# Two-stage attention with a gated convolution on one core: x in two layouts, float32 scores in column strips, block transposes, and the output product turned around

## The chip, the core and the metric

The kernel runs on one core of a Trainium2 chip. A core has five engines with queues of their own: PE multiplies matrices into PSUM (its weight loads are shown as PEld), DVE (VectorE) and ACT (ScalarE) work on SBUF and PSUM, POOL (GpSimd) on SBUF, and SP mostly issues transfers. Sixteen DMA engines carry the transfers that SP and ACT issue. Engines wait for one another through semaphores. The metric is the device time of one launch in microseconds (us); what the host does with inputs and outputs ahead of and behind the launch isn't in it.

## What is computed

x has 4 batches of 12,800 tokens with 128 channels in float32. With 32 learnt queries a summary h is drawn from x (phase one), each token then attends to the 32 rows of h (phase two), and the result goes through a causal convolution gate of five taps and two 128 by 128 products:

```python
def mab(q, kv):
    s = scale * (q @ kv.transpose(0, 2, 1))
    s = s - s.max(-1, keepdims=True)
    a = np.exp(s)
    a /= a.sum(-1, keepdims=True) + 1e-09
    return a @ kv
h = mab(I, x)
x = mab(x, h)
...
for k in range(K):
    gate_pre += conv_w[k][None, None, :] * xp[:, k:k + S, :]
gate = 1.0 / (1.0 + np.exp(-gate_pre))
val = x @ w_val
return (gate * val @ w_out).astype(np.float32)
```

Since each token's result is a mix of 32 rows, the taps and w_val are folded into weights of 32 rows (`wst`), and what the convolution reads is the table of probabilities.

## The kernel before

Tokens are dealt out so that a partition holds 100 neighbouring ones. A batch is cut into seven chunks of 8, 12 or 16 tokens a partition. In phase one, x is loaded (`load`), split into two float16 parts (`split1` L188 on ACT, `split2` L200 on DVE), and transposed, mostly by DMA (`trans_dma` L206, L209), partly by PE in the first batch. The scores with the queries (`scores`, L255 to L259) take a 128 by 128 tile of x as weights and 32 or 64 columns of queries as the moving side, two or three products for each tile; maximum, exponent and a second split follow, then the sums with x (`h_mm`). The functions `prep0` to `prep8` make from them the weights `wst` and the output weights `wo` of the batch.

Phase two of a chunk has the scores against h (`c_mm`), maximum, subtraction, exponent, sum and normalization (`c_max` to `c_norm`, POOL for L492 and L515), and four copies or parts of the float16 probabilities side by side (`c_hi`, `c_lo`, `c_dup`). These are transposed by PE (`y_mm`, L553) or by DMA (`y_t`, L544) into y, whose 128 rows are four blocks of 32: the probabilities, their low part, and copies. Two transfers (L579, L580) make z, a shifted copy of y, so that four products cover five taps.

The work that ends in the output is cut into 100 slots of 512 tokens, 25 a batch. A slot has four float16 gate products (`f_gate`, L589; three read y, one z), a value product (`f_val`, L596), tanh on ACT (`f_tanh`, L602), a multiplication on DVE (`f_gv`, L607), four float32 output products of 128 columns with g as weights (`f_out`, L613), and a copy and a store on ACT (`f_store`, L619, L620).

The order comes from due times: each function is put on a list with a time in units of a slot of 3.22 and the list is sorted; a scheduler then places the instructions, with some of them pinned behind others. The table that decides where a slot's steps stand against the next slot's is `F2`, with the steps gate, tanh, value, multiplication, output, store:

```python
for f, fn in zip(F2, (f_gate, f_tanh, f_val, f_gv, f_out, f_store)):
    at(t + f * SLOT, fn, b, c, q)
...
F2 = [-0.3, 0.23, 0.08, 0.87, 1.56, 2.08]
```

Of the kernel before, what the change touches and what calls it, by code (L numbers as in the profile page):

```python
# [10 lines left out]
F16 = mybir.dt.float16  # L11
# [10 lines left out]
NB = 100  # L22
TAPS = 5
HALO = TAPS - 1
SX = 64.0
SI = 64.0
SE = 4096.0
SH = 64.0
# [4 lines left out]

@with_exitstack
def tile_kernel(ctx: ExitStack, tc: tile.TileContext, x, inducing, w_val, conv_w, w_out, out):
    nc = tc.nc
    B = x.shape[0]
    SCALE = 1.0 / math.sqrt(P)
    V, S, T, G = nc.vector, nc.scalar, nc.tensor, nc.gpsimd

    xv = x.rearrange("b (p i) c -> b p i c", i=NB)
    ov = out.rearrange("b (p i) c -> b p i c", i=NB)

    chunks = [(0, 8), (8, 12)] + [(20 + 16 * g, 16) for g in range(5)]
    NCK = len(chunks)

    const = ctx.enter_context(tc.tile_pool(name="const", bufs=1))
    px = ctx.enter_context(tc.tile_pool(name="px", bufs=BUFS["XFB"]))
    pxs = ctx.enter_context(tc.tile_pool(name="pxs", bufs=BUFS["X12"]))
    pxt = ctx.enter_context(tc.tile_pool(name="pxt", bufs=BUFS["XT"]))  # L50
    pb = ctx.enter_context(tc.tile_pool(name="pb", bufs=2))
    p1 = ctx.enter_context(tc.tile_pool(name="p1", bufs=1))
    p2 = ctx.enter_context(tc.tile_pool(name="p2", bufs=2))
    p3 = ctx.enter_context(tc.tile_pool(name="p3", bufs=BUFS["P4B"]))
# [7 lines left out]
    def ps(role, shape, dt=F32):  # L62
        tag = PTAG[role]
        return psum.tile(shape, dt, name=role, tag=tag, bufs=PBUF[tag])

    def eng(op, b, c):
        return V if (ENG0 if b == 0 and c < 2 else ENG)[op] == "V" else G

    def copy(e, dst, src):
        if e == "S":  # L70
            S.copy(dst, src)
        else:
            (V if e == "V" else G).tensor_copy(dst, src)  # L73

    anchor = {}

    def pinned(e):
        if PIN and e in anchor:
            return tc.issue_after(anchor[e].ins)
        return contextlib.nullcontext()  # L80

    c_ = {}
    tpn = [0]
    st = {}
    bat = [dict() for _ in range(B)]
    xf_ = {}
    ys = {}
    zs = {}

    def constants():  # L90
        warm = const.tile([P, 1], F32, name="warm")
        V.memset(warm, 0.0)
        S.activation(warm, warm, AF.Exp)
        ident = const.tile([P, P], F16, name="ident")
        make_identity(nc, ident)
        identf = const.tile([P, P], F32, name="identf")
        make_identity(nc, identf)
        ones = const.tile([P, P], F32, name="ones")
        V.memset(ones, 1.0)
        ind = const.tile([M, P], F32, name="ind")  # L100
        nc.scalar.dma_start(ind, inducing)
        it = ps("t", [P, 512])
        T.transpose(it[:, :M], ind, identf[:M, :M])
        indT = const.tile([P, M], F32, name="indT")
        V.tensor_scalar(indT, it[:, :M], SI, None, ALU.mult)
        i12 = const.tile([P, 2, M], F16, name="i12")
        V.tensor_copy(i12[:, 0, :], indT)
        V.tensor_tensor(i12[:, 1, :], indT, i12[:, 0, :], ALU.subtract)
        iw = const.tile([P, M], F32, name="iw")
        V.tensor_scalar(iw, indT, SX, None, ALU.mult)  # L110
        w4 = const.tile([P, TAPS + 2, 4, M], F16, name="w4")
        G.memset(w4, 0.0)
        c_.update(w4=w4, ident=ident, identf=identf, ones=ones, i12=i12, iw=iw)

    def sched_f64(name, srcs, t, dt):
# [3 lines left out]
        def start():  # L119
            w["raw"] = p2.tile([P, k], I64, name=name + "_raw", tag="e", bufs=BUFS["EB"])  # L120
# [4 lines left out]
            w["w4"] = p2.tile([P, 4, k], I32, name=name + "_w4", tag="g", bufs=BUFS["TB"])  # L125
# [19 lines left out]
        at(t - 4, start)  # L145
# [8 lines left out]
    def halves(c):  # L154
        n = chunks[c][1]
        return {8: [(0, 8)], 12: [(0, 6), (6, 6)], 16: [(0, 8), (8, 8)]}[n]

    def half(b, c, i, kind):
        k = chunks[c][1] // len(halves(c))
        return st[b, c, i // k * k, kind], i % k  # L160

    def w1(b, c):
        return (W1 if b else W10)[c]

    def w2(b, c):
        return (W2 if b else W20)[c]

    def full(b, c):
        return b == 0 and PE_T0[c] == 2

    def load(b, c, q, m):
        if full(b, c) and len(wide) < BUFS["X12"]:
            wide.append((c, q))
            xf = pxs.tile([P, 8, P], F32, name="xw", tag="x12")
            st[b, c, q, "x"] = xf
        else:
            xf = px.tile([P, 8, P], F32, name="xf", tag="xf")
            if full(b, c):
                st[b, c, q, "x"] = xf
        dma = (nc.sync, nc.scalar, nc.gpsimd)[LQ[min(b, 1)]]  # L180
        for i, i0, k in [(0, NB - HALO, HALO), (HALO, 0, HALO)] if c == 0 else [(0, chunks[c][0] + q - HALO, m)]:
            dma.dma_start(xf[:, i:i + k, :], xv[b, :, i0:i0 + k, :])
        xf_[b, c, q] = xf

    def split1(b, c, q, m):
        x12 = st[b, c, q, "x"] = pxs.tile([P, 2, 8, P], F16, name="x12", tag="x12")
        with pinned("S"):
            S.mul(x12[:, 0, :m], xf_[b, c, q][:, :m], SX)  # L188

    def split2(b, c, q, m):  # L190
        xf, x1, x2 = xf_[b, c, q][:, :m], st[b, c, q, "x"][:, 0, :m], st[b, c, q, "x"][:, 1, :m]
        if (XP0, XP1, XP, XP)[b][2 * c + (1 if q else 0)]:
            if (XP0, XP1, XP, XP)[b][2 * c + (1 if q else 0)] == 2:
                S.mul(xf, xf, SX)
            else:
                G.tensor_scalar(xf, xf, SX, None, ALU.mult)
            G.tensor_tensor(x2, xf, x1, ALU.subtract)
            return
        with pinned("V"):
            V.scalar_tensor_tensor(x2, xf, SX, x1, ALU.mult, ALU.subtract)  # L200

    def trans_dma(b, c, q, m):
        xT = st[b, c, q, "T"] = pxt.tile([P, 2, 8, P], F16, name="xT", tag="xT")
        x12 = st[b, c, q, "x"]
        if m == 8:
            nc.sync.dma_start_transpose(xT.rearrange("p e i t -> p (e i) t"), x12.rearrange("p e i c -> p (e i c)"))  # L206
        else:
            for e in range(2):
                nc.sync.dma_start_transpose(xT[:, e, :m, :], x12[:, e, :m].rearrange("p i c -> p (i c)"))  # L209

    def trans_pe(b, c, q, m, e):
        if e == 0:
            st[b, c, q, "T"] = pxt.tile([P, 2, 8, P], F16, name="xT", tag="xT")
        tp = ps(XR[tpn[0] % len(XR)], [P, 8, P], F16)
        tpn[0] += 1
        for i in range(m):
            T.transpose(tp[:, i, :], st[b, c, q, "x"][:, e, i, :], c_["ident"])
        st[b, c, q, e] = tp

    def trans_evac(b, c, q, m, e):  # L220
        dst = st[b, c, q, "T"][:, e, :m, :]
        if e == 0:
            S.copy(dst, st[b, c, q, e][:, :m, :])
        else:
            V.tensor_copy(dst, st[b, c, q, e][:, :m, :])

    def trans_full(b, c, q, k, m):
        if k == 0:
            st[b, c, q, "T"] = pxt.tile([P, 8, P], F32, name="xTw", tag="xT")
        tp = ps(XR[tpn[0] % len(XR)], [P, 4, P])  # L230
        tpn[0] += 1
        for i in range(m):
            T.transpose(tp[:, i, :], xf_[b, c, q][:, k + i, :], c_["identf"])
        st[b, c, q, k] = tp

    def evac_full(b, c, q, k, m):
        dst, src = st[b, c, q, "T"][:, k:k + m, :], st[b, c, q, k][:, :m, :]
        if XE[2 * c + (1 if q else 0)][k // 4] == "S":
            S.copy(dst, src)
        else:  # L240
            V.tensor_copy(dst, src)

    def pieces(c):
        n = chunks[c][1]
        return {8: [(0, 8)], 12: [(0, 6), (6, 6)], 16: [(0, 8), (8, 8)]}[n]

    def scores(sc, b, c, q, m, rhs, rhsw, wide):
        for i in range(m):
            xT, k = half(b, c, q + i, "T")
            if full(b, c):  # L250
                T.matmul(sc[:, i, :M], xT[:, k, :], rhsw, start=True, stop=True)
                continue
            hi, lo = xT[:, 0, k, :], xT[:, 1, k, :]
            if wide:
                T.matmul(sc[:, i, :], hi, rhs.rearrange("p a j -> p (a j)"), start=True, stop=False)  # L255
            else:
                T.matmul(sc[:, i, :], hi, rhs[:, 1, :], start=True, stop=False)  # L257
                T.matmul(sc[:, i, :], hi, rhs[:, 0, :], start=False, stop=False)  # L258
            T.matmul(sc[:, i, :M], lo, rhs[:, 0, :], start=False, stop=True)  # L259

    def begin(b):
# [4 lines left out]
        if any(full(b, c) for c in range(NCK)):  # L266
            G.memset(d["h"], 0.0)
# [12 lines left out]
    def s1_add(b, c, q, m):  # L280
        s1 = st[b, c, "s1"][:, q:q + m, :]
        if full(b, c):
            return
# [534 lines left out]
```

## Time and profile before

| what | us |
|---|---|
| median of 3 runs (453.49 to 461.64) | 456.55 |
| span of the profiled execution, first to last instruction | 452.9 |
| PE busy, 0 to 80 us of the span | 49.96 (granted clock 0.68) |
| PE busy, 80 to 160 | 66.15 (0.96) |
| PE busy, 160 to 240 | 61.33 (0.91) |
| PE busy, 240 to 320 | 65.46 (0.96) |
| PE busy, 320 to 400 | 71.13 (0.96) |
| PE busy, 425 to 445 | 18.09 (0.91) |

The profile gives for the profiled execution its span; a time of its own with launch and end is not among what it shows, so the span is set against the runs. In the first 80 us the first batch's phase one runs. Then the output slots of a batch run beside phase one of the next, and from about 425 us on only the last slots are left. A row of a timeline has the start in the span, the duration, engine, line, operation, output and inputs, the shape, and in brackets how long the engine had been idle and what ended that. Rows of groups have the count after an x, then the busy time and the mean of one in ns. The granted clock is PE's, as a share of full speed. A matmul's end is modelled; back-to-back starts tell its cost better than its duration.

### The profile page before, as it was taken

Reading aid. Unit: us, or ns where it says so; the run is one execution under the profiler, and the core shown is the slowest. Engines: PE = TensorE matmul, PEld = TensorE weight load, DVE = VectorE, ACT = ScalarE, POOL = GpSimd, SP = SyncE. Lnnn points to the kernel's source line nnn. Section 1 sums busy time; section 2 is a strip of 40 time slices with the busy share of each in tenths; the row PEclk is TensorE's granted clock in tenths of the full one; section 3 lists DMA queues with packets and bytes.
Section 4 is the critical chain, followed back from the end, with each engine's and each line's share of the span. In section 5 each row is a group of like instructions: output and inputs, shape, how many; then the busy total and the mean of one; then the engine's idle time right before and its main releaser. Section 6 shows DMA issues by size and latency. Waiting matters only on the chain.

```text
span 452.9 us, 11587 instructions
## 1 busy us (share of the span) xinstructions
PE 355.6 (79%) x4597; PEld 274.8 (61%) x4597; DVE 346.0 (76%) x778; ACT 269.3 (59%) x454; POOL 216.1 (48%) x267
## 2 busy tenths in 40 slices
PE   3677656778899757887598868978779898988795
PEld 3576544557776545666386646756558676755463
DVE  4998899889877757997857878998939998665231
ACT  6667343486667535767555656676756566665353
POOL 2269827465865024584627313594737435462000
PEclk9666655799999988999979997999979999999898
DMA  8999539899999999999999798999997856789853
GB/s 290 255 236 201 112 77 204 205 250 257 240 245 200 171 166 233 242 235 230 203 241 272 187 198 173 289 243 243 229 211 178 172 155 163 158 186 224 178 162 117
DMA packets 137397, 93.18 MB, mean 206 GB/s; under 512 B 114016, under 2 KB 114304, under 8 KB 137344
## 3 DMA queue, kind: packets, MB, share of 16 engines
q1 hardware_dynamic: 121952, 65.94, 73.4%
q10 hardware_dynamic: 15392, 26.50, 17.9%
q8 instruction: 36, 0.59, 0.6%
q14 instruction: 17, 0.14, 0.1%
HBM read 26.50 MB, written 26.21 MB: 116 GB/s over the span
## 4 chain that ended last, share of the span: by engine, by line
DMA 39%; PE 27%; DVE 14%; POOL 7%; ACT 6%; issue 5%; SPq 1%; ACTq 0%; POOLq 0%; DVEq 0%
DMA xT<-x 19%; DMA z<-y 8%; PE g L589 7%; PE o L613 7%; DMA y<-p 6%; DMA out_dram<-os 4%; DVE x L200 2%; DVE g L607 2%; DMA xf<-in_x_dram 2%; PE v L596 2%; PE yp L553 2%; PE s L259 2%; ACT g L602 2%; PE s L255 1%; ACT x L188 1%
## 5 line engine op out<-in xcount | busy, mean ns | idle before, releaser
L613 PEld LDWEIGHTS o<-wo,g 128*128 128x128 f32 x800 | 106.5, 198 | 20.3 <-ACT os L619 7.3
L613 PE MATMUL o<-wo,g 128*128 128x128 f32 x800 | 114.2, 286 | 2.8 <-ACT os L619 1.7
L607 DVE SCALAR_TENSOR_TENSOR g<-g,v 128x512 f32<-128x512 f32 x100 | 67.7, 677 | 44.4 <-ACT g L602 33.6
L602 ACT ACTIVATE g<-g,gsc 128x512 f32<-128x512 f32 x100 | 68.8, 688 | 51.9 <-PE g L589 40.0
L619 ACT COPY os<-o 128x512 f32<-128x512 f32 x100 | 58.6, 586 | 56.2 <-PE o L613 41.7
L589 PE MATMUL g<-y,wst 128*128 128x512 f16 x296 | 83.0, 392 | 1.5 <-ACT g L602 1.5
L200 DVE SCALAR_TENSOR_TENSOR x<-xf,x 128x1024 f16<-128x1024 f32 (+1 forms) x51 | 70.8, 1396 | 1.0 <-ACT x L188 1.0
L589 PEld LDWEIGHTS <-wst 128*128 128x128 f16 x408 | 38.1, 100 | 46.6 <-DMA z<-y 17.5
L259 PEld LDWEIGHTS <-xT 128*128 128x128 f16 x800 | 59.2, 99 | 8.6 <-issue 4.2
L492 POOL TENSOR_TENSOR e<-e,m 128x512 f32<-128x512 f32 (+2 forms) x28 | 29.5, 1054 | 67.2 <-DVE m L486 61.7
L257 PE MATMUL s<-i,xT 128*128 128x32 f16 x356 | 33.9, 181 | 30.0 <-DMA xT<-x 28.9
L515 POOL TENSOR_TENSOR e<-e,z 128x512 f32<-128x512 f32 (+2 forms) x28 | 32.1, 1147 | 49.9 <-DVE z L507 33.2
L188 ACT ACTIVATE x<-xf 128x1024 f16<-128x1024 f32 (+1 forms) x52 | 52.1, 1019 | 5.7 <-DMA xf<-in_x_dram 5.5
L257 PEld LDWEIGHTS <-xT 128*128 128x128 f16 x404 | 33.1, 99 | 34.8 <-DMA xT<-x 32.1
L589 PE MATMUL g<-z,wst 128*128 128x512 f16 x92 | 36.2, 394 | 15.7 <-DMA z<-y 15.7
L530 POOL TENSOR_TENSOR p<-e,p 128x512 f16<-128x512 f32 (+2 forms) x28 | 36.4, 1301 | 19.2 <-DVE p L73 17.3
L596 PE MATMUL v<-y,wst 128*128 128x512 f16 x96 | 37.4, 390 | 6.1 <-DVE g L607 6.0
L307 POOL TENSOR_TENSOR s<-s,mb 128x512 f32<-128x512 f32 (+2 forms) x26 | 34.6, 1332 | 11.9 <-DVE mb L302 11.8
L255 PE MATMUL s<-h,xT 128*128 128x64 f16 x384 | 32.6, 196 | 3.3 <-DVE h L412 3.3
L258 PEld LDWEIGHTS <-xT 128*128 128x128 f16 x404 | 33.0, 99 | 3.0 <-issue 1.2
L259 PE MATMUL s<-i,xT 128*128 128x32 f16 x362 | 33.8, 180 | 0.3 <-DMA xT<-x 0.3
L258 PE MATMUL s<-i,xT 128*128 128x32 f16 x356 | 33.7, 180 | 0.0
(159 smaller groups left out, 763.5 us busy)
## 6 DMA issues: line engine op xcount, KB each, us to landing
out_dram<-os ACTq DMA_DIRECT2D x100, 256.0 KB, 4.0
xf<-in_x_dram SPq DMA_DIRECT2D x40, 512.0 KB, 5.4
z<-y SPq DMA_DIRECT2D x40, 256.0 KB, 4.4
xf<-in_x_dram SPq DMA_DIRECT2D x8, 384.0 KB, 4.5
xf<-in_x_dram SPq DMA_DIRECT2D x8, 256.0 KB, 4.2
z<-y SPq DMA_DIRECT2D x8, 192.0 KB, 4.1
xT<-x SPq DMA_TRANSPOSE x52, 5.8
y<-p SPq DMA_TRANSPOSE x11, 7.5
```

The source lines that it names most:

```text
L188: S.mul(x12[:, 0, :m], xf_[b, c, q][:, :m], SX)
L200: V.scalar_tensor_tensor(x2, xf, SX, x1, ALU.mult, ALU.subtract)
L255: T.matmul(sc[:, i, :], hi, rhs.rearrange("p a j -> p (a j)"), start=True, stop=False)
L257: T.matmul(sc[:, i, :], hi, rhs[:, 1, :], start=True, stop=False)
L258: T.matmul(sc[:, i, :], hi, rhs[:, 0, :], start=False, stop=False)
L259: T.matmul(sc[:, i, :M], lo, rhs[:, 0, :], start=False, stop=True)
L589: T.matmul(gp, d["wst"][:, k, :], r[:, q + o:q + o + 4, :].rearrange("p i t -> p (i t)"), start=i == 0, stop=i == len(taps) - 1)
L596: T.matmul(vp, d["wst"][:, 6, :], y[:, HALO + q:HALO + q + 4, :].rearrange("p i t -> p (i t)"), start=True, stop=True)
L602: anchor["S"] = S.activation(g, st[b, c, q, "g"], AF.Tanh, scale=bat[b]["gsc"])
L607: anchor["V"] = V.scalar_tensor_tensor(g, g, 1.0, st[b, c, q, "v"], ALU.add, ALU.mult)
L613: T.matmul(op[:, i, :], st[b, c, q, "gv"][:, i, :], bat[b]["wo"], start=True, stop=True)
L619: S.copy(os, st[b, c, q, "o"])
```

## The change

x is handed over twice: `xt` with channels in rows and tokens in columns, and `xk` in tiles of 128 tokens by 128 channels. The output is written with channels in rows. The layouts are made on the host. There are no splits and no transposes of x on the chip any more.

A batch is now six units of 2,048 tokens and one of 512. In both phases the scores are float32 products with the 32 queries (or the 32 rows of h) as weights and 512 tokens as the moving side; the four quarters of a unit go to four strips of 32 columns of PE, so that the result has queries and quarters in its 128 rows (`a_mm`, `b_mm`). In phase one maximum and sum are then along a row, the exponents are transposed by PE (`a_tr`) and multiplied with `xk`, again in four strips (`a_h`). In phase two DVE transposes blocks of 32 by 32 to get the queries along the row (`b_tr`) and back (`b_back`). The high and low float16 parts are laid into y by 16 transfers of 32 partitions a unit (`y_hi`, `y_lo`), and two more make z. The output product has `wo` as weights and 512 tokens as moving side, one product in place of four, and a store takes two slots.

There is no scheduler: the sorted list is the order on each engine, written out (`manual_schedule`). One unit of time is a slot. `LEAD` puts the scores of phase two six slots ahead of the slots that need them, and phase one of the next batch is spread among the slots of this one.

```diff
-    def f_out(b, c, q):
-        op = ps("o", [P, 4, P])
-        for i in range(4):
-            T.matmul(op[:, i, :], st[b, c, q, "gv"][:, i, :], bat[b]["wo"], start=True, stop=True)
-        st[b, c, q, "o"] = op
...
+    def a_mm(b, u):
+        w = UNITS[u][1]
+        sc = st[b, u, "s1"] = ps("s1", "s", [P, 512])
+        x = st[b, u, "xT"]
+        for g in range(G):
+            T.matmul(sc[M * g:M * g + M, :w], c_["iw"], x[:, w * g:w * g + w], start=True, stop=True, tile_position=(0, M * g))
...
+        for i in range(w // P):
+            T.transpose(et[:, i, :], st[b, u, "E"][:, P * i:P * i + P], c_["identf"])
...
+        for i in range(n):
+            for g in range(G):
+                T.matmul(hp[M * g:M * g + M, :], et[:, i, M * g:M * g + M], x[:, n * g + i, :],
+                         start=i == 0, stop=i == n - 1, tile_position=(0, M * g))
...
+    def b_mm(b, u):
+        w = UNITS[u][1]
+        sc = st[b, u, "s2"] = ps("s2", "s", [P, 512])
+        x = st[b, u, "xT"]
+        for g in range(G):
+            T.matmul(sc[M * g:M * g + M, :w], bat[b]["hq"], x[:, w * g:w * g + w], start=True, stop=True, tile_position=(0, M * g))
...
+    def b_tr(b, u):
+        w = UNITS[u][1]
+        s = st[b, u, "q"] = p2.tile([P, 16, M], F32, name="q", tag="q", bufs=3)
+        V.transpose(s[:, :w // M, :].rearrange("p i j -> p (i j)"), st[b, u, "s2"][:, :w])
...
+    def y_hi(b, u):
+        w = UNITS[u][1]
+        y, h = st[b, u, "y"], st[b, u, "hi"]
+        for blk, o in ((0, 4), (2, 4), (3, 6)):
+            for g in range(G):
+                nc.sync.dma_start(y[M * blk:M * blk + M, o + w * g:o + w * g + w], h[M * g:M * g + M, :w])
...
+        nc.sync.dma_start(z[:64, :n], y[:64, 0:n])
+        nc.sync.dma_start(z[64:, :n], y[:64, 1:n + 1])
...
+    def c_tanh(b, c):
+        g = st[b, c, "t"] = p2.tile([P, 512], F32, name="g", tag="gt", bufs=3)
+        S.activation(g, st[b, c, "g"], AF.Tanh, scale=bat[b]["gsc"])
...
+    def c_out(b, c):
+        op = st[b, c, "o"] = ps("o", "o", [P, 512])
+        T.matmul(op, bat[b]["wo"], st[b, c, "t"], start=True, stop=True)
...
+        for dt, fn in zip(CT, (c_gate, c_tanh, c_val, c_gv, c_out, c_ev)):
+            at(t + dt, fn, b, c)
...
+    with tc.manual_schedule():
...
+PBUF = dict(s=2, e=1, h=1, g=2, v=1, o=1)
+BUFS = dict(XT=10, XK=3, Y=3, Z=2, OS=2)
+LEAD = 6.0
...
+CT = [0, 0.3, 0.1, 0.6, 0.9, 1.25]
```

The order of PE at a slot's end, before. g_7182 are the gates of this slot; g_7175 is what tanh made of the gates of the slot ahead (g_7164):

```order
L589 MATMUL g_7182<-z4_7095,wst_6293 128x512
L596 LDWEIGHTS wst_6293
L596 MATMUL v_7191<-y_7074,wst_6293 128x512
L613 MATMUL o_7195<-wo_6299,g_7175 128x128 x4
L589 LDWEIGHTS wst_6293
L589 MATMUL g_7200<-y_7132,wst_6293 128x512
```

The output product reads what belongs to the slot ahead, and one slot's gates lie between a slot's own gates and its output product. The same place on PE in the new kernel; g_787 is what tanh makes of g_775, the gates just above:

```order
L372 MATMUL g_775<-zz_719,wst_485 128x512
L377 LDWEIGHTS wst_485
L377 MATMUL v_782<-y_664,wst_485 128x512
L389 MATMUL o_795<-g_787,wo_489 128x512
L372 LDWEIGHTS wst_485
L372 MATMUL g_797<-y_664,wst_485 128x512
```

The output product now reads its own slot's tanh and stands ahead of the next gates. Some slots have score work of the new kernel at this place on PE (s1 of the next batch's phase one, s2 of a later unit's phase two, four strips each):

```order
L377 LDWEIGHTS wst_485
L377 MATMUL v_817<-y_664,wst_485 128x512
L147 MATMUL s1_821<-xT_593,iw_99 32x512 x4
L389 MATMUL o_836<-g_828,wo_489 128x512
L285 MATMUL s2_838<-xT_118,hq_438 32x512 x4
L372 LDWEIGHTS wst_485
L372 MATMUL g_843<-y_664,wst_485 128x512
```

The s1 strips stand between value and output product, the s2 strips between the output product and the next gates. On SP a stretch of the middle of a batch reads like this before, where xT are transposes of x and z4 the shifted copy of y:

```order
L182 DMA xf_3680<-in_x_dram 128x1024
L579 DMA z4_3791<-y_3690 64x2048
L580 DMA z4_3791<-y_3690 64x2048
L206 DMA_TRANSPOSE xT_3774<-x12_3705 128x16x128
L206 DMA_TRANSPOSE xT_3800<-x12_3786 128x16x128
```

And so in the new kernel for one unit (hi and lo are the float16 parts):

```order
L140 DMA xk<-in_xk_dram 128x2048
L350 DMA y<-hi 32x512 x12
L356 DMA y<-lo 32x512 x4
L134 DMA xT<-in_xt_dram 128x2048
L362 DMA zz<-y 64x2048
L363 DMA zz<-y 64x2048
```

The transposes are gone, and 16 small transfers and a load stand on SP ahead of each z.

More of the change, by code (lines that the diff above doesn't have):

```diff
@@ L1 @@
-import contextlib
 import math
@@ L152, in conv_max @@
         c_.update(cmax=cmax, wval=c_["w1"][:, :P], cwT=c_["w1"][:, P:])
[L154 to L183, printed above, removed]
@@ L202, in trans_dma @@
[L202 to L218, printed above, removed]
@@ L220, in trans_evac @@
[L220 to L259, printed above, removed]
```

721 lines of the change are left out of this document (230 added, 491 removed).

## The prediction

> **What bounds the kernel now.** I read the page's busy times, then the chain of work that ended last, then the costliest groups, and last the timelines of the undisturbed end.
>
> ```profile
> span 452.9 us, 11587 instructions
> PE 355.6 (79%) x4597; PEld 274.8 (61%) x4597; DVE 346.0 (76%) x778; ACT 269.3 (59%) x454; POOL 216.1 (48%) x267
> DMA packets 137397, 93.18 MB, mean 206 GB/s; under 512 B 114016, under 2 KB 114304, under 8 KB 137344
> DMA 39%; PE 27%; DVE 14%; POOL 7%; ACT 6%; issue 5%; SPq 1%; ACTq 0%; POOLq 0%; DVEq 0%
> xT<-x SPq DMA_TRANSPOSE x52, 5.8
> L613 PE MATMUL o<-wo,g 128*128 128x128 f32 x800 | 114.2, 286 | 2.8 <-ACT os L619 1.7
> L589 PEld LDWEIGHTS <-wst x408: 95/98/181, 74.9 to 444.8; 128*128 128x128 f16 x136
> ```
>
> No engine is full. The path is a third transfers, most of them the DMA transposes of x, and a quarter PE. The first gate product of phase two is near 74.9 us, so 100 slots take about 3.75 us each up to 449 us. Also, L613 is called 400 times and shows 800 instructions: a float32 product runs as two halves.
>
> What would a slot cost without disturbance? The end of the program shows it, where only phase two is left (PE's timeline: start, duration):
>
> ```profile
> 430.31 1.05 PE L613 MATMUL o<-wo,g 128*128 128x128 f32 x8
> 431.20 0.81 PE L589 MATMUL g<-y,wst 128*128 128x512 f16 x3
> 431.85 0.38 PE L589 MATMUL g<-z,wst 128*128 128x512 f16 x1
> 432.06 0.38 PE L596 MATMUL v<-y,wst 128*128 128x512 f16 x1
> 432.28 1.05 PE L613 MATMUL o<-wo,g 128*128 128x128 f32 x8
> 433.19 0.81 PE L589 MATMUL g<-y,wst 128*128 128x512 f16 x3
> ```
>
> Gate to gate is 1.99 us and PE never pauses, since the output product between 432.28 and 433.19 belongs to the slot before: tanh and the multiplication of one slot run beside the gates of the next. So of 3.75 us, 1.76 are other work and waits.
>
> **The change, part by part.** *Removed:* splits, DMA transposes of x, PE and DMA transposes of the probabilities, float16 score products. They carry the waits above, and DVE and ACT get lighter: I cost what replaces them on these engines at nothing where it stands beside other work. The cover is PE's chain below; if it falls away, DVE has 100 multiplications of 0.69 and 25 units of some 4 us left, 169 us, and ACT 100 tanh and copies of 1.28 and 25 units of some 2.6, 193 us.
>
> *Moved: the output product.* In the new order each output product stands right behind its own slot's value product, and the next gates behind that (front part, order of PE). PE takes products in order, as here, where a gate waits for z (PE, then ACT and DVE behind it, and the last slot of the program):
>
> ```profile
> 423.26 0.81 PE L589 MATMUL g<-y,wst 128*128 128x512 f16 x3
> 426.24 0.39 PE L589 MATMUL g<-z,wst 128*128 128x512 f16 x1 [2.17 <-DMA z<-y]
> 426.46 0.58 PE L596 MATMUL v<-y,wst 128*128 128x512 f16 x1
> 426.83 1.92 PE L613 MATMUL o<-wo,g 128*128 128x128 f32 x8
> 426.66 0.69 ACT L602 ACTIVATE g<-g,gsc 128x512 f32<-128x512 f32 x1 [2.62 <-PE g L589]
> 427.38 0.69 DVE L607 SCALAR_TENSOR_TENSOR g<-g,v 128x512 f32<-128x512 f32 x1 [3.50 <-ACT g L602]
> 447.03 0.69 DVE L607 SCALAR_TENSOR_TENSOR g<-g,v 128x512 f32<-128x512 f32 x1 [2.19 <-ACT g L602]
> 447.87 1.13 PE L613 MATMUL o<-wo,g 128*128 128x128 f32 x8 [0.82 <-DVE g L607]
> ```
>
> The output product at 426.83 is that of the slot before: DVE had been idle since 423.88, so its input was ready for 2.9 us, and it stood behind the waiting gate. In the new kernel the wait for tanh and multiplication is added to every slot, and queued behind it are the next gates and all score work. The links, from these rows: first gate to last gate 0.65 (431.20 to 431.85), last gate to tanh 0.42, tanh to multiplication 0.72, its 0.69, then 0.15 to the output product (447.72 to 447.87), and 0.89 from that to the next gates (430.31 to 431.20): 3.52 us a slot. One float32 product of 512 columns costs what four of 128 did, as both stream 512. ACT adds a little, since the store's issue stands ahead of tanh:
>
> ```profile
> 439.31 1.05 PE L613 MATMUL o<-wo,g 128*128 128x128 f32 x8
> 440.20 0.81 PE L589 MATMUL g<-y,wst 128*128 128x512 f16 x3
> 440.40 0.59 ACT L619 COPY os<-o 128x512 f32<-128x512 f32 x1 [0.38 <-PE o L613]
> 441.02 0.34 ACTq L620 DMA_DIRECT2D out_dram<-os  x1
> 441.46 0.69 ACT L602 ACTIVATE g<-g,gsc 128x512 f32<-128x512 f32 x1 [0.47 <-PE v L596]
> ```
>
> Here tanh starts 1.26 after the gates (440.20 to 441.46) and not 1.07. Stores are now half as many: 0.1 a slot on average. Total 3.62 a slot, **362 us for 100**. In each slot PE is free from the end of the value product, 1.08 after the gates, to the output product at 2.63: a gap of 1.55 us.
>
> *Added: float32 scores in column strips.* A group (L147 or L285 of the new kernel) is four float32 products of 512 columns into 32 columns each; the group of L175 is sixteen of 128 columns. The trace has no such form. Ends: 0.89 if four strips run side by side, 3.56 if one after the other. In between, if the two halves of a product can't overlap and products start in order, the second half of a strip runs beside the first half of the next: 5 halves of 0.445, 2.2 us; for L175, 17 of 0.11, 1.9 us. I take these, as order is what the rows above show. The Trainium skill's "TensorE: Matmul & The Clock Gate" (Part 3, Measured speedup) has three column strips 2.38 times as fast as one after the other, which for four would be near 1.1 us a group by an estimate, nearer to the low end; no run here shows it.
>
> Where they stand, by the order of one batch in the middle: four whole b groups and the short one lie between output product and gates, so in full on the path; the others in the gap, where what is over 1.55 counts. Slot by slot (b and h 2.55, a 0.65, h 0.35, b and a 2.85, transposes and h 0.85, a and b behind the output 4.4, h 0.35, a and b 2.85, h 0.35, a 0.65, b and transposes 2.7, h 0.35, h and b of the short unit's place 2.7, preparation 1.85) that is 23 us. The first batch, part of whose work is ahead of the slots, has 16.5, the last, without the next batch's scores, 10.7: **73 us** in all. At the ends it is 21 and 151.
>
> *Added: 18 transfers a unit that lay out y and z.* SP issues them in order, with the loads between:
>
> ```profile
> L579 SPq DMA_DIRECT2D z<-y x24: 461/462/652, 81.3 to 430.8; - x24
> DMA to landing us min/median/max: 2.9/3.4/7.0
> L492 POOL TENSOR_TENSOR e<-e,m 128x512 f32<-128x512 f32 x20 | 23.4, 1171 | 22.1 <-DVE m L486 16.5 <-DVE z L506 5.4
> L515 POOL TENSOR_TENSOR e<-e,z 128x512 f32<-128x512 f32 x20 | 23.6, 1179 | 31.8 <-DVE z L507 16.8 <-DVE h L367 11.4 <-DVE mj L296 3.6
> L486 DVE TENSOR_REDUCE m<-e 128x16 f32<-128x512 f32 x20 | 13.5, 676 | 0.4 <-ACT e L475 0.3
> L497 ACT ACTIVATE e<-e 128x512 f32<-128x512 f32 x20 | 12.8, 638 | 4.6 <-POOL e L492 4.2 <-ACT os L619 0.4
> ```
>
> An issue is between 0.34 (ACT's above) and 0.46; I take the latter, since it is SP's. Scores to z, nothing in between: b 2.2, block transpose and its return about 0.65 each (between 0.6 and 0.7, as other DVE passes of 512), maximum 0.68, subtraction 1.17, exponent 0.64, sum 0.68 and two small ones 0.5, normalization 1.18, high part 0.6, together 9; sixteen issues 7.4, landing 3.4, two z issues 0.9, landing 3.4, together 15. So 24 to 26 us, against six slots of lead of about 4.4 = 26 to 28: hidden, by little. POOL's queue holds nothing else that waits. At the end of a batch the short unit doubles the issues: 36 by 0.46 = 16.6 us plus landings in four slots (17.6), for which I put 5 us at each of three boundaries, **15** (between 0 and 30).
>
> *The start.* SP's order puts 16.25 MB ahead of the last tile of phase one: six and a quarter units of 1.05 MB in two layouts, and three units of the next batch.
>
> ```profile
> GB/s 415 389 389 415 410 415 399 384 374 386 381 302 382 320 302 374 340 317 364 415 364 389 374 405 420 394 369 451 430 389 287 287 225 246 307 410 430 389 164 41
> DMA packets 1802, 2.85 MB, mean 356 GB/s; under 512 B 788, under 2 KB 1044, under 8 KB 1802
> 59.87 0.19 DVE L414 COPY hv<-t 128x32 f32<-128x32 f32 x1 [0.25 <-PE t L404]
> 65.98 0.93 PE L451 MATMUL t<-ident,w 128*128 128x128 f16 x7 [1.39 <-DVE w L447]
> ```
>
> At the mean of 356 GB/s (4 to 12 us of the trace, in 40 slices) that is 46 us, with 2 ahead of it **48**. From hv to the transposed weights 7 us with other DVE work between, and 2 to 3 for the sums ahead, **9**. Then the chain from scores to z, **25**. First gates at 82, between 70 (410 GB/s as in many slices, 42; 7; 21 with issues of 0.23, half for half the partitions) and 90 (the loads at 300).
>
> *The end:* from the end of the last output product's streaming (447.87 and 0.89, 448.8) to 452.9: **4**.
>
> **The sum:** 82 + 362 + 73 + 15 + 4 = 536 us of span. The span shown is 452.9 and the median of the runs 456.55; I add the same 4: **540 us**.
>
> **Rivals.** *Strips side by side:* 21 in place of 73, 488; six slots are then nearer to 24 us, so z may be late by up to 1 us a unit, 513. Against it speak the two halves of a product. The measurement named from the Trainium skill speaks for it. *One after the other:* 151 in place of 73, and 4 more at the start, 622; for it speaks only that no row here shows two products at once. *Short start and strips side by side:* 70 + 362 + 21 + 0 + 4 + 4 = 461, no change; it needs three terms at their low ends. *Faster: PE reaches past the waiting output product.* Then a slot is 1.99 again, and the score work fills PE: 199 + 25 groups b of 2.2 (55) + 18.75 units of a, h and transposes, 4.6 each (86) = 340 in place of 362 + 73, and 82 + 340 + 15 + 4 + 4 = 445. Its place is PE's queue, its price 1.5 us a slot, and it decides as soon as the order holds in more than one or two slots. Against it: the output product at 426.83, which waited though it was ready. *The clock.* If pauses halve it, gates and output cost 1.9 more a slot:
>
> ```profile
> 149.00:154.00 5.00, 2.46 (x45) 1.75 (x43) 3.10 (x17) 2.39 (x5) 0.00 (x0) 1.00 0.70 173
> ```
>
> With PE busy for 2.46 of 5 us the granted clock was still 1.00; a slot will have over 2 of 3.6 busy, so I leave this out but for the upper end. The Trainium skill's "TensorE: Matmul & The Clock Gate" (Why this matters for your kernels) asks for no pauses over about 3 us; by that rule gaps of 1.55 us don't halve it either, and the row agrees. *The change doesn't do what it says:* the order shows that the output products are where I said, so this has no chance of its own.
>
> **How the numbers follow.** Staggered strips as summed 0.50 (513 to 563 with the bounds of start and boundaries, 580 if z is late), side by side 0.21 (485 to 515), one after the other 0.17 (600 to 645), short start 0.06 (within 2%), PE reaching past the wait 0.06 (below 447). What a measurement here can tell from no change is about 2% (447 to 466). Faster 0.06, same 0.06, slower 0.88. The range of 484 to 625 leaves out these 0.12 at the low end and some 0.07 at the high one.
>
> **What would show it.** Slots "g v o" with nothing between should repeat each 3.5 to 3.7 us, PE waiting for DVE before the output product each time, 1.5 us where the gap is empty. The starts of the four products of L147 tell 0.9, 2.2 or 3.6 us. First gates should be near 82 us, and PE should wait for transfers of z only near the batch boundaries. I am wrong if slots run under 3 us, if a group costs 1 us, or if the gates wait for z in every unit.

## The result, and the profile after

| | median us (lowest to highest) | ratio to before (95%) |
|---|---|---|
| before | 458.34 (453.49 to 461.64, 4 runs) | |
| after | 649.94 (643.51 to 656.81, 4 runs) | 1.420 (1.405 to 1.436) |

The kernel is 42% slower. The ratio goes by the runs at the higher granted clock alone, so it isn't quite that of the two medians. The page of its profiled execution (engines with busy time and instructions; the granted clock in 40 slices; the chain that ended last, by engine and by line; two groups):

```profile
span 646.3 us, 6632 instructions
PE 401.3 (62%) x2161; PEld 154.3 (24%) x2161; DVE 198.7 (31%) x479; ACT 189.9 (29%) x346; POOL 92.5 (14%) x145
PEclk9655666889779977797785985969897968889789
DMA 30%; SPq 25%; PE 24%; DVE 8%; ACT 6%; issue 5%; POOL 1%; ACTq 0%; POOLq 0%; DVEq 0%
SPq L350 18%; DMA zz<-y 16%; PE o L389 8%; PE g L372 7%; SPq L356 5%; DMA y<-lo 5%; DVE g L385 3%; DMA out_dram<-os 3%; ACT g L381 3%; PE h L175 3%; DMA w_raw<-in_moe_conv_w_dram 3%; PE s L147 2%; DMA xk<-in_xk_dram 2%; SPq L362 2%; PE s L285 1%
L372 PE MATMUL g<-zz,wst 128*128 128x512 f16 x100 | 44.4, 444 | 96.6 <-DMA zz<-y 96.6
L389 PE MATMUL o<-g,wo 128*128 128x512 f32 x200 | 131.1, 742 | 85.3 <-DVE g L385 85.3
```

Instructions fell from 11,587 to 6,632 and every engine but PE has less to do. A quarter of the path is now SP's queue, the time in which it only *issues* transfers (L350 and L356, which lay out y), and 16% the landing of z. The gate products that read z waited 96.6 us in all, 24 times: in nearly every one of the 28 units.

PE's timeline at the end, where phase one is over, and in the middle (start, duration, instruction, idle time ahead of it):

```profile
614.63 0.82 PE L372 MATMUL g<-y,wst 128*128 128x512 f16 x3
617.17 1.12 PE L389 MATMUL o<-g,wo 128*128 128x512 f32 x2 [1.28 <-DVE g L385]
618.13 0.81 PE L372 MATMUL g<-y,wst 128*128 128x512 f16 x3
...
302.86 1.06 PE L285 MATMUL s<-xT,hq 128*32 128x512 f32 x8
303.86 0.82 PE L372 MATMUL g<-y,wst 128*128 128x512 f16 x3
305.05 1.08 PE L175 MATMUL h<-xk,ET 128*32 128x128 f32 x32
```

An undisturbed slot takes 3.50 us (614.63 to 618.13), with the wait for DVE ahead of the output product. The group of L285, eight half products in four strips, takes 1.00 us (302.86 to 303.86), and so does that of L175 nearly: the strips run side by side.

### The profile page after: what moved, and what is told of

The parts are those of the page before. It is cut to its first block, busy times and chain, and to the rows that moved or that the text cites. A ratio compares the mean times of both kernels' runs of the same rounds, so it can differ in the third digit from the quotient of the medians.

```text
span 646.3 us, 6632 instructions
## 1 busy us (share of the span) xinstructions
PE 401.3 (62%) x2161; PEld 154.3 (24%) x2161; DVE 198.7 (31%) x479; ACT 189.9 (29%) x346; POOL 92.5 (14%) x145
## 4 chain that ended last, share of the span: by engine, by line
DMA 30%; SPq 25%; PE 24%; DVE 8%; ACT 6%; issue 5%; POOL 1%; ACTq 0%; POOLq 0%; DVEq 0%
SPq L350 18%; DMA zz<-y 16%; PE o L389 8%; PE g L372 7%; SPq L356 5%; DMA y<-lo 5%; DVE g L385 3%; DMA out_dram<-os 3%; ACT g L381 3%; PE h L175 3%; DMA w_raw<-in_moe_conv_w_dram 3%; PE s L147 2%; DMA xk<-in_xk_dram 2%; SPq L362 2%; PE s L285 1%
## 5 line engine op out<-in xcount | busy, mean ns | idle before, releaser
L389 PE MATMUL o<-g,wo 128*128 128x512 f32 x200 | 131.1, 742 | 85.3 <-DVE g L385 85.3
L372 PE MATMUL g<-zz,wst 128*128 128x512 f16 x100 | 44.4, 444 | 96.6 <-DMA zz<-y 96.6
L300 POOL TENSOR_TENSOR q<-q,m 128x512 f32<-128x512 f32 (+1 forms) x28 | 26.8, 956 | 312.0 <-DVE m L295 312.0
L389 PEld LDWEIGHTS o<-g,wo 128*128 128x128 f32 x200 | 33.9, 213 | 134.4 <-DVE g L385 133.4
L332 POOL TENSOR_TENSOR lo<-p,hi 128x512 f16<-128x512 f32 (+1 forms) x28 | 29.4, 1051 | 116.5 <-issue 77.9
L175 PE MATMUL h<-xk,ET 128*32 128x128 f32 x800 | 37.7, 344 | 11.3 <-DMA xk<-in_xk_dram 9.3
L317 POOL TENSOR_TENSOR q<-q,z 128x512 f32<-128x512 f32 (+1 forms) x28 | 26.8, 956 | 98.1 <-DVE z L312 69.1
L147 PE MATMUL s<-xT,iw 128*32 128x512 f32 (+1 forms) x224 | 35.2, 708 | 0.3 <-DVE iw L80 0.3
L175 PEld LDWEIGHTS h<-xk,ET 128*32 128x32 f32 x800 | 27.7, 137 | 30.6 <-issue 19.9
L285 PE MATMUL s<-xT,hq 128*32 128x512 f32 (+1 forms) x224 | 30.0, 612 | 0.0
L322 DVE STREAM_TRANSPOSE p<-q 128x512 f32<-128x512 f32 (+1 forms) x28 | 18.2, 650 | 22.1 <-POOL q L317 21.4
```

What stands on the lines that cost most here:

```text
L147: T.matmul(sc[M * g:M * g + M, :w], c_["iw"], x[:, w * g:w * g + w], start=True, stop=True, tile_position=(0, M * g))
L175: T.matmul(hp[M * g:M * g + M, :], et[:, i, M * g:M * g + M], x[:, n * g + i, :], start=i == 0, stop=i == n - 1, tile_position=(0, M * g))
L285: T.matmul(sc[M * g:M * g + M, :w], bat[b]["hq"], x[:, w * g:w * g + w], start=True, stop=True, tile_position=(0, M * g))
L372: T.matmul(gp, d["wst"][:, k, :], r[:, o + s:o + s + CH], start=i == 0, stop=i == len(taps) - 1)
L389: T.matmul(op, bat[b]["wo"], st[b, c, "t"], start=True, stop=True)
```

## Why z is late: the loop

One turn near the end, with no loads in flight (DVE, PE, ACT, SP and PE again), and a row of SP's waits (us in total, times, longest):

```profile
603.33 0.71 DVE L322 STREAM_TRANSPOSE p<-q 128x512 f32<-128x512 f32 x1 [1.23 <-POOL q L317]
605.82 0.61 PE L372 MATMUL g<-zz,wst 128*128 128x512 f16 x1 [2.98 <-DMA zz<-y]
606.47 0.69 ACT L381 ACTIVATE g<-g,gsc 128x512 f32<-128x512 f32 x1 [3.65 <-PE g L372]
607.05 0.61 ACT L327 CAST hi<-p 128x512 f16<-128x512 f32 x1
607.69 7.51 SPq L350 DMA_DIRECT2D y<-hi  x12
615.30 2.75 SPq L356 DMA_DIRECT2D y<-lo  x4
619.37 0.50 SPq L362 DMA_DIRECT2D zz<-y  x1
619.92 0.59 SPq L363 DMA_DIRECT2D zz<-y  x1
623.98 0.39 PE L372 MATMUL g<-zz,wst 128*128 128x512 f16 x1 [1.54 <-DMA zz<-y]
...
SPq L350 <- ACT hi L327: 121.8, 21, 12.8
```

The first gates of a unit wait for its z (605.82). In ACT's order the high part of the *next* unit's probabilities (L327) stands right behind the tanh of these very gates, so it starts only now (607.05), though its input p was ready at 604.04. Then come sixteen issues (10.3 us), the landing of y (1.3), two issues of z (1.1) and its landing (3.5): the next unit's z is there at 623.98, 18.2 us after its predecessor. Four undisturbed slots take 14.0. The lead of six slots is counted from the scores; from L327 it is only 3.1 slots, and they are counted in slots that themselves wait. So one late unit makes the next one late. In all, SP waited 121.8 us for such high parts.

## The experiments

All times below are medians beside runs of the kernel before on the same chip (454 to 462 us). The last column is PE's total wait of the gates for z.

| run | us | ratio (95%) | wait for z, us |
|---|---|---|---|
| changed kernel | 649.9 | 1.420 (1.405 to 1.436) | 96.6 |
| e1_lead | 569.2 | 1.246 (1.226 to 1.266) | 30.5 |
| e2_wide | 545.5 | 1.194 (1.170 to 1.218) | 21.2 |
| e3_pipe | 684.5 | 1.498 (1.469 to 1.527) | 152.5 |
| e4_wload | 650.6 | 1.424 (1.401 to 1.447) | 99.3 |
| e5_lead_wide | 513.5 | 1.116 (1.093 to 1.138) | 0 |
| e6_lead_wide_pipe | 440.5 | 0.957 (0.942 to 0.972) | 1.1 |
| e7_lead_pipe | 561.7 | 1.220 (1.201 to 1.239) | 92.1 |
| e8a_copy | 501.0 | 1.088 (1.071 to 1.106) | 0 |
| e13_split | 469.1 | 1.028 (1.009 to 1.047) | 15.9 |
| e10_shift | 504.8 | 1.110 (1.102 to 1.118) | 0 |
| e11_start | 507.4 | 1.115 (1.105 to 1.125) | 0 |
| e12_retime | 427.9 | 0.938 (0.926 to 0.951) | 0 |
| e14_start2 | 412.4 | 0.910 (0.904 to 0.916) | 0 |

**The lead, the issues, and the output product, each alone.**

```diff
-BUFS = dict(XT=10, XK=3, Y=3, Z=2, OS=2)
-LEAD = 6.0
+BUFS = dict(XT=10, XK=3, Y=3, Z=3, OS=2)
+LEAD = 10.0
...
-AS = -8.0
+AS = -11.0
```

> LEAD 6 to 10 slots (three z buffers, phase one of the next batch 3 slots earlier), so that the high parts of a unit are ready before the first gates of the unit ahead. Theory A (z is late because the chain tanh of a unit's first slot, high part, 16 issues on SP, z, first slot of the next unit closes on itself, some 18 to 20 us a unit): the waits of PE for z, 97 us, go nearly all, a unit takes what SP's 18 issues and 2 loads need, about 14.5 us, and the span is 500 to 530 us. Rival B (SP's own rate with its waits is the limit, 20 us a unit whatever the lead): 620 to 650 us. Rival C (PE's chain and strips are the loss, z only shows it): over 600 us with z's waits gone.

```diff
-            for g in range(G):
-                nc.sync.dma_start(y[M * blk:M * blk + M, o + w * g:o + w * g + w], h[M * g:M * g + M, :w])
+            nc.sync.dma_start(y[M * blk:M * blk + M, o:o + G * w], h[M * blk:M * blk + M, :G * w])
```

> Lead as in the changed kernel, but one transfer of 32 rows and 2048 columns for each block of y (4 a unit in place of 16); it leaves out the gathering of the four strips, so y holds the wrong tokens. Theory A: 12 issues of 0.62 us less in the closed chain, 7.5 us a unit, which brings a unit from 20 to its own 15 us: 500 to 530 us. Rival B' (landing of transfers behind 1 MB loads is the long part, not the issues): over 590 us. Rival C: over 600 us.

```diff
-CT = [0, 0.3, 0.1, 0.6, 0.9, 1.25]
+CT = [0, 0.3, 0.1, 0.6, 1.15, 1.5]
```

> Output product behind the next slot's gates and value product (0.9 to 1.15, copy 1.25 to 1.5), nothing else. If the closed chain over z sets the time, a slot's saved 1.5 us is mostly lost in the wait for z: 600 to 640 us, and PE waits longer for z. If the wait for tanh and multiplication in each slot sets it, 100 times 1.5 us go: about 500 us.

The longer lead wins 81 us and comes out between theory A (500 to 530) and rival B (620 to 650), since both are partly true. SP's wait for the high parts falls from 121.8 to 4.6 us: the loop is open. Now SP's queue (of e1_lead) has hardly a pause left:

```profile
280.30 0.88 SPq L140 DMA_DIRECT2D xk<-in_xk_dram  x1
281.23 13.23 SPq L350 DMA_DIRECT2D y<-hi  x12
294.55 2.44 SPq L356 DMA_DIRECT2D y<-lo  x4
297.09 0.53 SPq L134 DMA_DIRECT2D xT<-in_xt_dram  x1
298.35 0.50 SPq L362 DMA_DIRECT2D zz<-y  x1
298.90 0.89 SPq L363 DMA_DIRECT2D zz<-y  x1
299.83 0.61 SPq L140 DMA_DIRECT2D xk<-in_xk_dram  x1
300.54 14.88 SPq L350 DMA_DIRECT2D y<-hi  x12
...
518.59 10.01 SPq L350 DMA_DIRECT2D y<-hi  x12
533.81 8.38 SPq L350 DMA_DIRECT2D y<-hi  x12
```

A unit is 19 us apart (281.23 to 300.54), and 15.2 in the last batch, where no loads stand between: twelve issues there take 8 to 10 us, with a load right ahead of them 10 to 17. So the limit is both, loop and issue rate. One transfer a block instead of four, with the old lead, shortens the longest piece of the loop but leaves it closed: the gates still wait 21.2 us for z, and 545 is over the 500 to 530 of a loop without sixteen issues. Moving the output product back behind the next gates, alone, makes it *slower*: slots next to each other fall to 1.95 us, but the chain of the unit gets longer (e3_pipe, PE and ACT):

```profile
330.63 0.82 PE L372 MATMUL g<-y,wst 128*128 128x512 f16 x3
332.58 0.81 PE L372 MATMUL g<-y,wst 128*128 128x512 f16 x3
...
300.33 0.69 ACT L381 ACTIVATE g<-g,gsc 128x512 f32<-128x512 f32 x1 [8.87 <-PE g L372]
302.47 0.59 ACT L395 COPY os<-o 128x512 f32<-128x512 f32 x1 [1.45 <-PE o L389]
303.62 0.62 ACT L327 CAST hi<-p 128x512 f16<-128x512 f32 x1 [0.56 <-DMA xk<-in_xk_dram]
```

The copy of the output product now stands between tanh (300.33) and the high part (303.62): 3.3 us from the one to the other instead of 0.6, and with that the wait for z grows from 96.6 to 152.5; the gates that read y wait 62.1 us more for its low part. My expectation of 600 to 640 was wrong for this reason: the wait in the loop bounds, so shorter slots win nothing, and the move made the loop longer.

**Together.** The next four kernels combine these; e5 and e6 have the wide transfers.

> The changed kernel with both limits on z taken away together: the shifted copy is issued ten slots ahead of the gates instead of six, and each block of y is filled by one transfer instead of four (left out: the gathering of the four strips into one row block, so the numbers are not the reference's). Theory A (z is held by a loop that closes through the issue queue; its length is latency plus sixteen issues): with 4 + 2 issues a unit the queue needs about 5 us of the 17 to 18 us that four slots and a unit's strips take on TensorE, so z is in time, the slots run at 3.5 us all through, and the time is 100 for the start, 352 for a hundred slots, 21 to 30 for strips and boundaries and about 8 at the end: 475 to 500 us. Rival C (the slots themselves are longer with strips between them, or the granted clock stays low whether z waits or not): over 530 us.

> The run before it, with the output product put back behind the next slot's gates, as it stood in the kernel before (left out: the same gathering of strips). Theory A: once z is in time TensorE's chain of 3.5 us a slot is what bounds, and taking the round over ScalarE and VectorE out of it brings a slot to about 2.5 to 2.8 us: 100 + 265 + 30 + 8, 380 to 430 us. Rival (something else, such as the loads of x or the order of ScalarE, bounds near 480): within 3% of the run before it.

> The changed kernel with the ten-slot lead and with the output product behind the next slot's gates, all sixteen transfers of y kept; nothing is left out. Theory A: the issue queue needs 16 x 0.7 to 0.9 us and the loads and z besides, about 17 to 19 us a unit, and bounds alone: 540 to 590 us, like the ten-slot lead without the move (569). Rival (the chain of a slot was what bounded that run): 430 to 490 us.

```diff
-        for blk, o in ((0, 4), (2, 4), (3, 6)):
-            for g in range(G):
-                nc.sync.dma_start(y[M * blk:M * blk + M, o + w * g:o + w * g + w], h[M * g:M * g + M, :w])
+        for g in range(G):
+            nc.sync.dma_start(y[:M, 4 + w * g:4 + w * g + w], h[M * g:M * g + M, :w])
...
+        nc.sync.dma_start(y[64:96, 4:4 + n], y[:M, 4:4 + n])
+        nc.sync.dma_start(y[96:, 6:6 + n], y[:M, 4:4 + n])
```

> The run before it with 12 issues a unit for y and z in place of 18: the third and fourth blocks of y are copied from the first in one transfer each once that has landed; the three small weight matrices are also loaded first. Nothing is left out, and the same bytes are written. Theory A (the number of issues bounds): 12 issues of 0.7 to 1.0 us plus two loads, 10 to 13 us a unit, under the slots' 11 to 13: 430 to 490 us, near the kernel before. Rival B (bytes or the collision of the transfers with the loads bounds, not their number): over 540 us, as the run before it.

With z in time (e5) the kernel takes 514 us, a little over the 475 to 500 expected, and moving the output product back then wins 73 us (e6): 0.7 us a slot, where it lost 35 before. At 440 us e6 is over its 380 to 430 too; what holds it there was not tried. With all sixteen issues kept (e7, beside e1_lead) the same move brings 569 to 562, nothing that the intervals tell apart. e8a has the same bytes in 12 issues for 18 (and the weights' loads first) and wins 61 against e7, but misses its 430 to 490: its copies stand on SP behind the two transfers of z, which wait 23.9 us in all for y to land, and `DMA y<-y` is 20% of its chain.

**Is it the queue or the transfers?** e13_split leaves e7 as it is and lets GpSimd issue eight of the sixteen:

```diff
-                nc.sync.dma_start(y[M * blk:M * blk + M, o + w * g:o + w * g + w], h[M * g:M * g + M, :w])
+                (nc.gpsimd if blk == 3 else nc.sync).dma_start(y[M * blk:M * blk + M, o + w * g:o + w * g + w], h[M * g:M * g + M, :w])
...
-            nc.sync.dma_start(y[M:2 * M, 4 + w * g:4 + w * g + w], l[M * g:M * g + M, :w])
+            nc.gpsimd.dma_start(y[M:2 * M, 4 + w * g:4 + w * g + w], l[M * g:M * g + M, :w])
```

> The run with the ten-slot lead and the moved output product (561.7, sixteen transfers of y on one queue), with eight of the sixteen issued by GpSimd instead; the same transfers, bytes and order else. Nothing is left out. Theory A (the rate of one issue queue bounds): 8 + 2 issues a unit on SP, and GpSimd has time left for eight unless one costs it over 1 us: 440 to 500 us. Rival B (the transfers themselves or the DMA engines bound): 540 us or more.

Same transfers, same bytes, 561.7 to 469.1 us. GpSimd's timeline and PE's wait:

```profile
313.27 2.01 POOL L350 DMA_DIRECT2D y<-hi  x4 [3.67 <-issue]
316.79 1.99 POOL L356 DMA_DIRECT2D y<-lo  x4 [0.29 <-POOL lo L332]
...
PE g L372 <- DMA zz<-y: 15.9, 6, 6.5
```

An issue costs GpSimd 0.50 us, and the wait for z falls from 92.1 to 15.9. The rate of one queue was the limit, not the transfers. The Trainium skill's "DMA: Bandwidth & Descriptors" (Issuing engines are not separate DMA queues) says that issuing from several engines saves only the sequencer's time, which is usually small against the transfer. The first half agrees; here the time saved was what bounded.

**A kernel without the gathering.** The last block transposes can write the four strips side by side, and ACT and POOL can write y from there:

```diff
-        V.transpose(p[:, :w], st[b, u, "q"][:, :w // M, :].rearrange("p i j -> p (i j)"))
+        for g in range(G):
+            V.transpose(p[:, w * g:w * g + w], q[M * g:M * g + M, :w // M, :].rearrange("p i j -> p (i j)"))
...
+        S.copy(st[b, u, "y"][:M, 4:4 + n], st[b, u, "p"][:, :n])
+        Gp.tensor_tensor(y[M:2 * M, 4:4 + n], st[b, u, "p"][:, :n], y[:M, 4:4 + n], ALU.subtract)
```

> The changed kernel without the twelve transfers that gather the strips: the last block transposes write the four strips side by side into rows 0 to 31 (four instructions instead of one on VectorE), ScalarE and GpSimd then write the first two blocks of y straight from there (2048 columns on 32 partitions each), and two transfers copy the first block to the third and fourth. Two plus two issues a unit are left of eighteen. Lead of ten slots, output product behind the next slot's gates. Nothing is left out. Theory A (transfers in the issue queue are what the change costs): like the run with wide transfers and the moved product, 440, plus 1.4 us a unit on ScalarE and 2 on VectorE where these are late: 435 to 475 us. Rival (the ScalarE and VectorE work that takes their place bounds): over 490 us.

It took 504.8, over its expectation. z was never late, but four transposes in a row (start, duration) now stood ahead of a slot's multiplication, and PE waited for that (e10_shift, DVE and PE's waits):

```profile
333.98 2.84 DVE L324 STREAM_TRANSPOSE p<-q 32x512 f32<-32x512 f32 x4 [1.23 <-POOL q L317]
336.85 0.69 DVE L379 SCALAR_TENSOR_TENSOR g<-g,v 128x512 f32<-128x512 f32 x1
...
PE v L371 <- DVE g L379: 47.4, 20, 4.9
```

e12_retime spreads the same work, two transposes behind each of two multiplications (at 383.98 and 386.14, for one unit), not behind four as I wrote beforehand. A slot more of lead, an earlier phase one and writes in two halves belong to it:

```diff
+BT = [(0.25, "b_mm"), (0.7, "b_tr"), (0.72, "b_max"), (0.75, "b_sub"), (1.65, "b_exp"), (1.95, "b_sum"), (2.0, "b_norm"),
+      (2.65, "b_back", 0), (2.7, "b_back", 1), (3.65, "b_back", 2), (3.7, "b_back", 3), (3.5, "y_begin"), (3.6, "b_hi", 0), (4.6, "b_hi", 1),
+      (4.1, "b_lo", 0), (5.3, "b_lo", 1), (5.05, "y_hi"), (6.1, "z_dma")]
+LEAD = 11.0
```

> The run without the gathering transfers (504.8), with only the order of its work changed: the four block transposes of a unit stand behind four different slots' VectorE products instead of all together ahead of one (there they take 2.84 us and TensorE waits 47 us for that product), the 2048-column writes of ScalarE and GpSimd are done in two halves, and each step of the two softmax passes stands behind the tanh and copy of its slot. Nothing is left out. If those stalls were the rest of its time, ScalarE's and VectorE's own work bounds at some 10 to 11 us a unit: 430 to 465 us. Rival (their own work plus the start bounds already): 490 to 510 us.

427.9 us: 77 won by these together, with the same work. That wait is 13.0 us now, and slots next to each other take 1.95 us (PE, the starts of their gates):

```profile
388.32 0.82 PE L366 MATMUL g<-y,wst 128*128 128x512 f16 x3
390.27 0.81 PE L366 MATMUL g<-y,wst 128*128 128x512 f16 x3
392.21 0.81 PE L366 MATMUL g<-y,wst 128*128 128x512 f16 x3
```

**The start.** e4_wload issues the loads of the weights first; e11_start is e10 with the first batch's tiles ahead of the next batch's and a fourth buffer for `xk`; e14_start2 is e12 with both.

```diff
-        at(t - 0.5, start)
+        at(-950, start)
```

> The three weight loads are issued on ACT at the very start, with buffers of their own. The chain shows 22 us behind them between 22 and 47 us. If they delay the start, first gates at 75 to 85 us in place of 96.8, and the span 12 to 22 us shorter, 625 to 634. If the loads of x hold it anyway, the same.

```diff
-        at(-900.5 + n, load_t, n // NU, n % NU)
+        at(-900.5 + n if n < NU else -A0 * NU - LEAD - PREP + A0 * 3 + AT[5] + 0.5 + 0.01 * n, load_t, n // NU, n % NU)
```

> The run before it with the loads of the first batch in another order: its seven blocks of both layouts first, the first three of the second batch behind them, and four buffers in place of three for the second layout. Nothing is left out. If the start (100 us before the first gate that reads the shifted copy, against 82 predicted) comes from 3 MB that stand ahead of what the first pass reads, it gets 5 to 9 us shorter and the time falls by as much; if the first pass is held by its own chain, or the loads' total is what counts, no change of more than 3 us.

> The retimed run (427.9) with both edits of the start together: the three small weight matrices are loaded ahead of x into buffers of their own, and the first batch's seven blocks of both layouts are loaded ahead of the second batch's first three. Nothing is left out. If the weights and the order of the loads hid each other, the sums of phase one are ready near 50 us and not near 59, and the first gates come 8 to 11 us earlier: 415 to 421 us. If the start is held by its own chain on VectorE and ScalarE, less than 3 us: 425 us or more.

Alone neither moved the total by more than 3 us: in e4 PE still waited for `xk` (until 39.13, and until 38.63 without the edit), in e11 DVE for the weights, whose transfer had now come behind the loads:

```profile
39.13 1.94 PE L175 MATMUL h<-xk,ET 128*32 128x128 f32 x32 [8.72 <-DMA xk<-in_xk_dram]
```

```profile
55.01 0.23 DVE L103 TENSOR_SCALAR w_w<-w_raw 128x128 int32<-128x128 int32 x1 [6.82 <-DMA w_raw<-in_moe_w_out_dram]
```

Together they bring the first gates from 101.37 us (e12) to 86.84, more than the 8 to 11 expected, and the kernel to 412.4 us, 9% under the kernel before. Two waits that end close to each other hide one another's price; each alone was tried on other kernels, not on e12.

## Why the prediction was right and wrong

Right was the direction, slower with 0.88, and for the reason given: with z in time the kernel is still 12% slower (e5), and with the output product put back 4% faster (e6). The time, 650 where 540 was forecast, lies outside the range of 484 to 625.

*The slot, right:* 3.52 predicted, 3.62 with a store ahead of tanh; 3.50 measured, 3.63 where a store stood ahead of tanh (631.87 to 635.50). It waits for tanh and multiplication in each slot, and the rival in which PE reaches past the output product is out. The price of that move, 1.5 us a slot, is too high as a net cost: 73 us by e5 and e6. PE stands idle ahead of the output product for 85.3 us here and 90.9 in e5; score work fills the rest of the gap.

*The step that failed:* "24 to 26 us, against six slots of lead of about 4.4 = 26 to 28: hidden, by little." The margin was measured from the scores, as if the slots ran on. But ACT takes its work in order, and the high part of the next unit stands behind a tanh that itself waits for z; the loop above is what the six slots became, and with ten slots 66 of the 96.6 us go (e1_lead). I had asked what stands behind a waiting instruction on PE, and said of POOL's queue that nothing there waits; ACT's I did not follow. The issue was also dearer, 0.63 us on average and not 0.46 (7.51 for twelve): 2.7 us a unit. So the chain was too long for its lead even without the loop: the first unit, with no gates ahead of it, took 29.3 us from its scores (72.44) to the gate that reads z (101.76). z cost 97 us where I had put 15, all at the boundaries.

*The strips, right side not taken:* five staggered halves, 2.2 us, were the main case; 1.00 is measured, near the low end of 0.89, with 21 in place of 73 us by the prediction's own count. One product alone takes 0.96 in the new form (617.17 to 618.13), not the 0.89 of four short ones. The estimate of 1.1 from the Trainium skill's "TensorE: Matmul & The Clock Gate" (Part 3, Measured speedup) was nearer than my reading of the two halves. This rival's allowance for z, up to 1 us a unit, was the same mistake: 96.6 in 24 waits is 4.0.

*The clock, left out:* I kept half speed for the upper end, since gaps of 1.55 us would not cause it. The gaps of a slot didn't; the waits for z did:

```profile
119.57 0.82 PE L372 MATMUL g<-y,wst 128*128 128x512 f16 x3
126.69 0.61 PE L372 MATMUL g<-zz,wst 128*128 128x512 f16 x1 [6.29 <-DMA zz<-y]
...
314.80 0.39 PE L372 MATMUL g<-zz,wst 128*128 128x512 f16 x1 [3.13 <-DMA zz<-y]
316.69 2.07 PE L389 MATMUL o<-g,wo 128*128 128x512 f32 x2 [1.29 <-DVE g L385]
...
625.87 1.84 PE L389 MATMUL o<-g,wo 128*128 128x512 f32 x2 [1.28 <-DVE g L385]
627.50 1.49 PE L372 MATMUL g<-y,wst 128*128 128x512 f16 x3
```

Behind a pause of 6.29 us a product takes 0.61 in place of 0.39. Behind the one of 3.13 the first product is still fast, but at 315.5 the granted clock falls from 1.00 to 0.50, and the output product takes 2.07 in place of 1.12. At 626.1 it falls behind two pauses of 1.54 and 1.28 us. The Trainium skill's "TensorE: Matmul & The Clock Gate" (Why this matters for your kernels) puts it near 3 us of pause; the pauses of 6.29 and 3.13 agree, those of 1.54 and 1.28 show that shorter ones do it too. In this trace the clock changes only at instants that lie whole multiples of 3.41 us apart (315.54, 605.67, 612.50, 626.15, 629.56). Of the 115 stretches between them at full clock, 22 are followed by half clock: in 21 of these PE was busy for at most 1.6 us, in the other 93 for 1.55 or more (busy as the profile models it). An undisturbed slot stays above that with 1.8 to 2.2 us a stretch. The prediction's row, 2.46 busy in 5 us, is 1.68 in 3.41, just above it, and tells nothing of the waits. The same 2,161 products kept PE busy for 401.3 us here, 357.0 in e5 and 330.6 in e14: 44 to 71 us more. How much of that lay on the path no run separates.

*The start, too short:* 82 predicted; first gates at 96.8, 15 more. The last sums of phase one came at 57.8 and not at 48, and the way from them to the first scores of phase two (72.4) took 14.7 and not 9. The weights' transfer, which the prediction left out, held DVE until 38.75, and a tile of the first batch, behind tiles of the next, held PE until 38.63. In the retimed kernel the two orders of loading together are worth 14.5.

The sum with measured terms: 540 + 82 (z beyond the 15) + 15 (start) − 52 (strips) + 44 to 71 (clock) = 629 to 656, against 650. The terms come from different runs; that they add up doesn't show that each lies whole on the path. One reading ahead of the sum was off as well, and nothing rests on it: the transposes of x are 19 of the 39% of transfers on the path before, half and not most.

## What to carry to other kernels

A lead counted in steps covers a chain only if no link of the chain stands, on any in-order engine, behind work of the step that waits for it: follow each link to its queue, and count the lead from the last such link. Count transfers by their issues on one queue as well as by bytes; many small ones can bound a kernel whose DMA engines are half free (busy for 0.37 to 0.56 behind the start here), and a second queue or fewer pieces then helps (92 us by e13, 61 by e8a). A move that is good by itself can be worth nothing or less until the bound ahead of it is gone, so try edits together as well as alone.

## What was not expected of the hardware

- Four float32 products of 512 columns in four column strips take 1.00 us together (0.96 for one alone): the two halves of each don't keep the strips apart.
- An issue of a 32 KB transfer within SP's queue takes 0.59 us at the median of L350 and up to 2.1, and twelve in a row took 8 to 10 us without a load right ahead of them in the queue and 10 to 17 with one (e1_lead). Why was not tried.
- GpSimd issued the same kind of transfer in 0.50 us (e13_split).
- The granted clock changed only at multiples of 3.41 us, by how long PE had been busy in the stretch before and not by one pause (the changed kernel).
